# Later checks of converted slices, two slots for the first quarter sums, and undivided reciprocal copies in a fused attention and Fourier-mixing kernel

## The chip, the cores and the metric

The kernel runs on one core of one Trainium2 chip. The metric is the device time of one execution in microseconds; the number for a kernel is the median of its runs. One execution was also recorded by the hardware profiler, which gives the trace and the profile.

## The reference, cut to what matters

Two blocks follow each other. The first is an attention in which a query sees only the keys of its own hash bucket; the second mixes by a Fourier transform over sequence and channels, normalizes, and applies two dense layers.

```python
# attention: q, k, v are (4, 8, 768, 64), proj is (64, 6)
q_bits = (einsum('bhsd,dk->bhsk', q, proj) > 0); k_bits = ...
mask = q_bucket[:, :, :, None] == k_bucket[:, :, None, :]
scores = where(mask, q @ k.T / sqrt(64), -1e9)
attn = exp(scores - max); attn = attn / (sum(attn) + 1e-9)
x = (attn @ v), heads side by side            # (4, 768, 512)
# mixing: w_ch1 is (512, 2048), w_ch2 is (2048, 512), given as 64-bit floats
u = x + real(fft(fft(x, axis=1), axis=2))
un = (u - mean(u)) / sqrt(var(u) + 1e-6)
out = u + relu(un @ w_ch1) @ w_ch2
```

## The kernel before, in words

There are four batches, and each has four pairs of heads, numbered n = 0 to 15. While the attention of batch b runs, the mixing of batch b - 1 runs in its gaps: the main loop (L1567 on) steps through `attention(b)` chunk by chunk and advances the generator `other`, which is `mix(b - 1)`, in proportion. So TensorE has matmuls of both at hand. The part that the change touches is the attention of batch 1 (pairs 4 to 7) beside the mixing of batch 0, and within it the preparation of the weights that all later batches use.

**Attention of a pair.** The keys come in six chunks of 128 (`scores`, `weights`, `weigh`, `values`). For a chunk TensorE makes two score tiles (L905), ScalarE takes their exponential into one of two buffers `pk0` and `pk1` (L916), VectorE multiplies each head by the bucket mask (L930), VectorE adds the chunk to the running sum `acc` (L1026, in `tally`), and TensorE multiplies by the values (L941). When a pair's six chunks are through, `scale` makes the reciprocals of the row sums: a matmul over ones (L960), a transpose (L967), an addition and a reciprocal (L969, L970), eight small copies on ScalarE that put the reciprocals into place (L978, tile `rr`), another transpose (L983) and a multiplication of the pair's output (L987). In batch 1 the eight copies are made in two groups of four, one chunk apart, and each group is put behind the last exponential, mask or sum that was issued.

**Anchors.** `in_turn()` issues what stands under it after the instructions that `done_by` remembers, one for ScalarE and one for VectorE. Else a scheduler of the framework orders the instructions of all batches but the first by its own priorities. The first batch's attention has its order written out.

**The first dense layer.** `mlp7` uses a seven-product scheme in place of eight. The 2048 columns of `w1` are taken as 8 steps f, and for each f `quarters(f)` makes four sums of quarters of `w1` on VectorE: s1 (L1249), s2 (L1250), s3 (L1251) and s4 (L1252) in four slots of the tile `tq`, and stores the seven factors to DRAM (tile `ad`, L1254 and L1255) for the later batches. `inner` (L1466 on) then makes the seven products of f: A11 and A12 into bank p1, S2 into p6, S1 and S4 into p5, S3 and A22 into p7 (all L1456). Two PSUM banks serve these four names in turn in batches 0 to 2, so each product waits for a copy of ScalarE: L1478 and L1485 read p1, L1481 reads p6, L1488 and L1497 read p5, L1493 and L1505 read p7. VectorE adds them up (L1482, L1489, L1494, L1498, L1506), ScalarE applies the rectifier (L1495, L1499, L1507). `quarters(f + 1)` is called at the end of step f.

**The second dense layer.** `outer7` does the same for the other layer, three times two row blocks j for each half of the hidden columns (L1335), with sums on VectorE (L1320, L1321, L1355, L1363, L1347, L1381 to L1387) and copies on ScalarE (L1354, L1365, L1368); its temporaries are slots 0 to 2 and 3 to 5 of the same tile `tq`, in turn.

**The conversion of w2.** `weights2` runs beside the mixing of batch 0 and turns 16 slices of 64-bit `w_ch2` into 32-bit floats. `Arrival.convert(i)` calls `narrow`: two VectorE operations on the high words (L639, L643), one ScalarE operation on the low words (L647), two additions on VectorE (L652), and then a check on ScalarE of whether any value is too small (L654 and L655, which ends with the reading of an accumulated sum). The check overwrites the raw slice. Then `fetch(i + 2)` loads the next slice into the same one of two raw slots, from the GpSimd queue (L704). After every second slice VectorE makes four sums of the pair (L1301 to L1304), and after eight slices the half is stored to DRAM (`bd`, L1306).

Of the kernel before, what the change touches and what calls it, by code (L numbers as in the profile page):

```python
# [20 lines left out]
P = 128  # L21
# [464 lines left out]
def _main(  # L486
# [141 lines left out]
    def narrow(dst, raw, col, low=None):  # L628


        lo, hi = (raw[..., i] for i in range(2))
        t = lo.bitcast(F32)
        if low is None:

            low, t = lo, hi.bitcast(F32)
        di = dst.bitcast(I32)


        nc.vector.tensor_scalar(  # L639
            di, hi, 3, (1 << 30) - 1,  # L640
            op0=ALU.logical_shift_left, op1=ALU.bitwise_and,
        )
        nc.vector.scalar_tensor_tensor(  # L643
            di, hi, -(1 << 30), di, op0=ALU.bitwise_and, op1=ALU.bitwise_or
        )

        nc.scalar.activation(low, lo.bitcast(U32), AF.Copy, scale=2.0**-29)  # L647
        if len(di.shape) == 2:
            nc.vector.tensor_tensor(di, di, low, op=ALU.add)
        else:  # L650
            for i in range(di.shape[1]):
                nc.vector.tensor_tensor(di[:, i], di[:, i], low[:, i], op=ALU.add)  # L652

        nc.scalar.activation(t, hi, AF.Abs)  # L654
        nc.scalar.activation(  # L655
            t, t, AF.Relu, bias=least, scale=-1.0, accum_out=strange[:, col : col + 1]
        )
# [33 lines left out]
    class Arrival:  # L691


        def __init__(self, slices, raws, col, queue):
            self.slices, self.raws, self.col, self.queue = slices, raws, col, queue
            self.wide = slices[0][1].dtype == I64
# [14 lines left out]
        def convert(self, i, low=None):  # L711
            if self.wide:
# [6 lines left out]
                narrow(dst, raw, self.col + i, low)  # L719
            self.fetch(i + self.depth)  # L720
# [226 lines left out]
    def scale(n, oos, sums):  # L947
# [25 lines left out]
        apart = NPAIR <= n < TWO  # L973
        for g in range(2):
            with in_turn() if apart else nullcontext():
                for i in range(4):
                    j = 2 * g + i // 2
                    nc.scalar.copy(  # L978
                        rr[32 * i : 32 * i + 32, g], rc[32 * j : 32 * j + 32]
                    )  # L980
            if apart and g == 0:
                yield
# [6 lines left out]
    def attention(b):  # L989
# [11 lines left out]
        for t in range(NPAIR):  # L1001
# [12 lines left out]
            def tally(c, pk, sums):  # L1014
# [8 lines left out]
                else:  # L1023

                    for g in (0, 1) if b == 0 else (slice(0, 2),):
                        done_by[ET.DVE] = nc.vector.tensor_tensor(  # L1026
# [41 lines left out]
        for sc in scales:  # L1068
            if next(sc, True) is None:
                yield  # L1070
                next(sc, None)
# [170 lines left out]
    def quarters(f):  # L1242

        st = tq[:, 0:4].rearrange("p i (k m) -> p i k m", m=P)
# [3 lines left out]
        s2, s1, s3, s4 = (st[:, i] for i in range(4))  # L1248
# [6 lines left out]
        nc.sync.dma_start(ad[f, 3:7].rearrange("i p k m -> p i k m"), st)  # L1255
# [17 lines left out]

    def weights2():
# [13 lines left out]
        arrival = Arrival(slices, [zt2[:, i] for i in range(2)], NDC * DFF // WC, nc.gpsimd)  # L1288
        for half in range(2):
# [4 lines left out]
            for i in range(HF):  # L1294
                with in_turn():
                    arrival.convert(half * HF + i)
                yield
                if i % 2:
                    b11, b21, b22, t4, t1, t2, t3 = (q[:, i // 2] for q in right7)
                    with in_turn():  # L1300
                        nc.vector.tensor_tensor(t3, b22, t1, op=ALU.subtract)  # L1301
                        nc.vector.tensor_tensor(t1, t1, b11, op=ALU.subtract)
                        nc.vector.tensor_tensor(t2, b22, t1, op=ALU.subtract)
                        nc.vector.tensor_tensor(t4, b21, t2, op=ALU.subtract)  # L1304
# [93 lines left out]
    def mlp7(b):  # L1398
# [46 lines left out]
        def product(i, ps, start=True):  # L1445
            n = done[0]
            left = ring[n % NR]
            if b == 0:
                f = n // 7
                if i >= S2:  # L1450
                    left = tq[:, i - S2].rearrange("p (k m) -> p k m", m=P)
# [61 lines left out]
        for half in range(2):  # L1513
            if b == 0 and half:
                quarters(HF // 2)
            for i, _ in enumerate(inner(half)):
                if b == 0 and half and i % 3 < 2:
                    next(arrival2, None)
                yield
# [9 lines left out]
    def after(n, one, two):  # L1529

        for i, _ in enumerate(one):
            if i >= n and (i - n) % 2 == 0:
                next(two, None)
            yield
# [124 lines left out]
```

## Time and profile before

| what | number |
|---|---|
| median of three runs | 1079.54 us |
| lowest and highest | 1077.59 and 1079.67 us |
| the profiled execution | 1079.54 us, of which the span is 1077.8 us |
| TensorE busy | 1034.6 us (96%) |
| VectorE busy | 786.7 us (73%) |
| ScalarE busy | 500.4 us (46%) |
| GpSimd busy | 59.3 us (5%) |
| check of a w2 slice, three instructions of L654 and L655 | 688, 776 and 190 ns |
| one reciprocal copy (L978) | 197 ns |
| one quarter sum or pair sum (L1249 to L1252, L1301 to L1304) | 417 to 420 ns |

The profile names engines PE (TensorE matmul), PEld (its weight load), DVE (VectorE), ACT (ScalarE), POOL (GpSimd) and SP (SyncE). A row gives a source line, an operation, the tiles written and read, and a duration; what stands in brackets is how long the engine was idle before it, and which instruction ended the wait. Instructions overlap at their ends, so rows that follow each other start closer together than their durations say.

### The profile page before, as it was taken

What the parts mean: (1) busy time and instruction counts of PE and PEld (TensorE: products, weight loads), DVE (VectorE), ACT (ScalarE), POOL (GpSimd) and SP (SyncE); (2) the same over time, 40 slices, a digit from 0 to 9 for tenths busy, and PEclk for the clock granted to TensorE, in tenths of its full rate; (3) what the DMA queues carried; (4) which work ended last, traced back from release to release, by engine and by line L of the source; (5) the groups of instructions that cost most, each with busy time, mean ns of one, the idle gap of its engine ahead of it and who ended that gap; (6) DMA issues with size and microseconds to landing.
All of it is one profiled execution on the core that took longest, in us unless ns stands there. A gap on an engine that the chain in (4) does not pass through costs nothing.

```text
span 1077.8 us, 14130 instructions
## 1 busy us (share of the span) xinstructions
PE 1034.6 (96%) x4933; PEld 633.4 (59%) x4933; DVE 786.7 (73%) x1336; ACT 500.4 (46%) x1055; POOL 59.3 (5%) x132
## 2 busy tenths in 40 slices
PE   7989899999999999999999999999999999999997
PEld 3333364447644585545664575645675579668576
DVE  5899969896789977777858876776856875644353
ACT  6988554762287323455336424354325522440420
POOL 0000000011000020010000020010000012200000
PEclk9999999999999999999999999999999999999998
DMA  8764452370154461224062233222033204222301
GB/s 200 206 141 78 99 143 54 122 237 9 29 131 169 136 187 37 52 64 88 11 191 73 64 104 116 50 66 66 15 111 96 69 23 173 61 78 90 125 20 42
DMA packets 175710, 103.13 MB, mean 96 GB/s; under 512 B 129552, under 2 KB 162960, under 8 KB 175632
## 3 DMA queue, kind: packets, MB, share of 16 engines
q1 hardware_dynamic: 169840, 88.65, 30.6%
q0 software_dynamic: 4224, 13.11, 3.7%
q8 instruction: 41, 0.67, 0.3%
q10 hardware_dynamic: 1568, 0.39, 0.2%
q14 instruction: 37, 0.30, 0.1%
HBM read 81.14 MB, written 20.97 MB: 95 GB/s over the span
## 4 chain that ended last, share of the span: by engine, by line
PE 72%; DVE 17%; ACT 6%; issue 2%; DMA 1%; SPq 1%; DVEq 0%; ACTq 0%
PE o L1335 26%; PE h_p L1456 22%; PE oo L941 8%; PE sc L905 7%; DVE acc L1026 3%; DVE pk L930 2%; PE cs L1147 2%; ACT pk L916 2%; PE A L1176 2%; PE B L1176 1%; DMA kn<-in_k_dram 1%; ACT rr L978 1%; DVE x L1190 1%; PE sum L960 1%; SPq L576 1%
## 5 line engine op out<-in xcount | busy, mean ns | idle before, releaser
L1335 PE MATMUL o<-w,h 128*128 128x256 f32 x1152 | 260.0, 383 | 0.8 <-DVE w L1347 0.6
L1335 PEld LDWEIGHTS o<-w,h 128*128 128x128 f32 x1152 | 217.8, 191 | 41.8 <-issue 6.5
L916 ACT ACTIVATE pk<-sc 128x768 f32<-128x768 f32 x192 | 147.4, 809 | 78.2 <-PE oo L941 33.3
L1456 PE MATMUL h_p<-x,w 128*128 128x384 f32 x448 | 164.5, 494 | 3.1 <-ACT h L1478 1.6
L905 PE MATMUL sc<-qt,kt 64*128 64x384 f32 x768 | 154.9, 505 | 3.1 <-ACT pk L916 2.8
L930 DVE SCALAR_TENSOR_TENSOR pk<-qb,kb,pk 128x768 f32<-128x768 bf16 x132 | 128.7, 1012 | 39.0 <-ACT pk L916 38.4
L941 PE MATMUL oo<-pk,vn 128*64 128x385 f32 (+1 forms) x768 | 146.4, 495 | 1.1 <-DVE pk L930 0.6
L1456 PEld LDWEIGHTS h_p<-x,w 128*128 128x128 f32 x448 | 82.0, 190 | 69.3 <-issue 9.9
L1026 DVE TENSOR_TENSOR acc<-acc,pk 128x1536 f32<-128x1536 f32 (+1 forms) x72 | 105.8, 1483 | 5.3 <-ACT pk L916 5.1
L1456 PE MATMUL h_p<-w 128*128 128x384 f32 x288 | 106.1, 490 | 0.1
L941 PEld LDWEIGHTS oo<-pk,vn 128*64 128x64 f32 x768 | 50.5, 136 | 87.0 <-issue 72.6
L905 PEld LDWEIGHTS sc<-qt,kt 64*128 64x128 f32 x768 | 66.5, 187 | 55.7 <-issue 18.4
L1456 PEld LDWEIGHTS h_p<-w 128*128 128x128 f32 x288 | 53.6, 190 | 39.6 <-ACT w L1493 2.4
L1365 ACT COPY tq<-o 128x256 f32<-128x256 f32 x24 | 8.9, 373 | 104.8 <-PE o L1335 104.8
L1347 DVE SCALAR_TENSOR_TENSOR w<-o,rs,w 128x256 f32<-128x256 f32 x56 | 26.6, 479 | 41.2 <-PE o L1335 41.2
L1335 PE MATMUL o<-w 128*128 128x256 f32 x176 | 42.2, 383 | 0.2 <-DVE w L1347 0.2
L1489 DVE TENSOR_TENSOR h<-h 128x384 f32<-128x384 f32 x32 | 17.8, 555 | 29.6 <-ACT h L1488 29.6
L1085 POOL DMA_DIRECT2D out_dram<-w x30 | 16.4, 548 | 407.6 <-issue 314.6
L1335 PEld LDWEIGHTS o<-w 128*128 128x128 f32 x176 | 32.9, 190 | 7.5 <-DVE w L1347 1.2
L1354 ACT COPY tq<-o 128x256 f32<-128x256 f32 x24 | 8.8, 368 | 60.3 <-PE o L1335 60.1
L1381 DVE TENSOR_TENSOR tq<-tq,o 128x256 f32<-128x256 f32 x24 | 10.0, 418 | 36.4 <-PE o L1335 36.4
L1482 DVE TENSOR_TENSOR h<-h 128x384 f32<-128x384 f32 x32 | 17.7, 552 | 21.8 <-ACT h L1481 21.7
(170 smaller groups left out, 1334.5 us busy)
## 6 DMA issues: line engine op xcount, KB each, us to landing
w<-ad SPq DMA_DIRECT2D x168, 128.0 KB, 2.0
w<-bd SPq DMA_DIRECT2D x42, 512.0 KB, 4.4
zraw<-in_moe_w_ch_dram POOLq DMA_DIRECT2D x16, 512.0 KB, 4.4
bd<-w SPq DMA_DIRECT2D x14, 512.0 KB, 3.3
vn<-in_v_dram SPq DMA_DIRECT2D x32, 192.0 KB, 3.5
qn<-in_q_dram SPq DMA_DIRECT2D x120, 48.0 KB, 2.4
kn<-in_k_dram SPq DMA_DIRECT2D x60, 96.0 KB, 3.0
zraw<-in_moe_w_ch_dram SPq DMA_DIRECT2D x8, 512.0 KB, 7.4
```

The costliest lines, as they stand in the source:

```text
L905: last[0] = nc.tensor.matmul(ps[:, h, 0:HALF], kt[rows, ks], qt[rows, qs], start=kb is not None, stop=True,)
L916: done_by[ET.Activation] = nc.scalar.activation(pk[:, g, :, 0:HALF], ps[:, :, 0:HALF], AF.Exp, scale=SCALE)
L930: done_by[ET.DVE] = nc.vector.scalar_tensor_tensor(w, qb[:, h].rearrange("p (g s) -> p g s", g=2), kb[:, h, c : c + 1], w, op0=ALU.is_equa ...
L941: oo = nc.tensor.matmul(oos[g][h * D : (h + 1) * D, 0:w], nat["v", n][:, (2 * c + h) * D : (2 * c + h + 1) * D], pk[:, g, h, 0:w], start=( ...
L1026: done_by[ET.DVE] = nc.vector.tensor_tensor(acc[:, g], (first if c == 1 else acc)[:, g], new[:, g], op=ALU.add,)
L1147: nc.tensor.matmul(ps[:, pc + 2 * lo : pc + 2 * hi - 1 : 2], z[:, cp, pc, par, t * P : (t + 1) * P], ch[:, cp, pc, lo:hi], start=(cp == 0) ...
L1176: nc.tensor.matmul(ps[:, cols], F[:, par, k, t, j * P : (j + 1) * P], sq[:, t, k, cols], start=(t == 0), stop=(t == 1),)
L1335: nc.tensor.matmul(ps, a[:, r], right7[i][:, r], start=start and r == 0, stop=r == HF // 2 - 1, skip_group_check=not start,)
L1347: nc.vector.scalar_tensor_tensor(t[:, cols], src, r, t[:, cols], op0=ALU.mult, op1=ALU.add)
L1456: nc.tensor.matmul(ps, left[:, k], right[i][:, k], start=start and k == 0, stop=k == 1, skip_group_check=not start,)
L1482: done_by[ET.DVE] = nc.vector.tensor_tensor(c21, c12, c21, op=ALU.add)
L1489: done_by[ET.DVE] = nc.vector.tensor_tensor(c22, c21, c22, op=ALU.add)
```

## The change

It has three parts. The check of a converted `w2` slice and the fetch that follows it are no longer made with the conversion but kept as `rest` and made by `settle()`, which is called before the next conversion or at the mixing step after it; the four sums of a pair of slices lose their anchor. The first two sums of `quarters` use slots 0 and 1 of `tq` for even f and slots 4 and 5 for odd f, where the four sums of an odd f are stored by two transfers in place of one. And the eight reciprocal copies of a pair of batch 1 are issued in one step and without an anchor, as they are in the other batches; the additions into `acc` are no longer remembered in `done_by`.

```diff
@@ -651,10 +651,13 @@
             for i in range(di.shape[1]):
                 nc.vector.tensor_tensor(di[:, i], di[:, i], low[:, i], op=ALU.add)
 
-        nc.scalar.activation(t, hi, AF.Abs)
-        nc.scalar.activation(
-            t, t, AF.Relu, bias=least, scale=-1.0, accum_out=strange[:, col : col + 1]
-        )
+        def check():
+            nc.scalar.activation(t, hi, AF.Abs)
+            nc.scalar.activation(
+                t, t, AF.Relu, bias=least, scale=-1.0, accum_out=strange[:, col : col + 1]
+            )
+
+        return check
 
     def average(f):
 
@@ -693,6 +696,7 @@
 
         def __init__(self, slices, raws, col, queue):
             self.slices, self.raws, self.col, self.queue = slices, raws, col, queue
+            self.rest = None
             self.wide = slices[0][1].dtype == I64
             self.depth = len(raws) if self.wide else 4
 
@@ -708,7 +712,8 @@
                         dst, src if len(dst.shape) == 2 else src.rearrange("p (s n) -> p s n", n=n)
                     )
 
-        def convert(self, i, low=None):
+        def convert(self, i, low=None, later=False):
+            check = None
             if self.wide:
                 dst = self.slices[i][0]
                 raw = self.raws[i % self.depth].bitcast(I32)
@@ -716,8 +721,23 @@
                     raw = raw.rearrange("p (n w) -> p n w", w=2)
                 else:
                     raw = raw.rearrange("p (s n w) -> p s n w", w=2, n=dst.shape[-1])
-                narrow(dst, raw, self.col + i, low)
-            self.fetch(i + self.depth)
+                check = narrow(dst, raw, self.col + i, low)
+
+            def rest():
+                if check:
+                    check()
+                self.fetch(i + self.depth)
+
+            if later:
+                self.rest = rest
+            else:
+                rest()
+
+        def settle(self):
+            if self.rest:
+                with in_turn():
+                    self.rest()
+                self.rest = None
 
     def weights1():
         slices = [
@@ -970,16 +990,10 @@
         nc.vector.reciprocal(rc, rc)
         yield
         rr = wt([P, 2, HALF // 32], F32, "rr", f"rr{n}")
-        apart = NPAIR <= n < TWO
         for g in range(2):
-            with in_turn() if apart else nullcontext():
-                for i in range(4):
-                    j = 2 * g + i // 2
-                    nc.scalar.copy(
-                        rr[32 * i : 32 * i + 32, g], rc[32 * j : 32 * j + 32]
-                    )
-            if apart and g == 0:
-                yield
+            for i in range(4):
+                j = 2 * g + i // 2
+                nc.scalar.copy(rr[32 * i : 32 * i + 32, g], rc[32 * j : 32 * j + 32])
         nc.vector.transpose(
             rt.rearrange("p (j i) -> p j i", i=32),
             rr.rearrange("p g j -> p (g j)")[:, :, None].broadcast_to([P, S // 32, 32]),
@@ -1023,7 +1037,7 @@
                 else:
 
                     for g in (0, 1) if b == 0 else (slice(0, 2),):
-                        done_by[ET.DVE] = nc.vector.tensor_tensor(
+                        nc.vector.tensor_tensor(
                             acc[:, g], (first if c == 1 else acc)[:, g], new[:, g],
                             op=ALU.add,
                         )
@@ -1066,9 +1080,7 @@
         while pending:
             finish()
         for sc in scales:
-            if next(sc, True) is None:
-                yield
-                next(sc, None)
+            next(sc, None)
 
 
     HW = HALF // 2
@@ -1241,18 +1253,23 @@
 
     def quarters(f):
 
-        st = tq[:, 0:4].rearrange("p i (k m) -> p i k m", m=P)
+        st = tq.rearrange("p i (k m) -> p i k m", m=P)
         (a11, a12), (a21, a22) = (
             [w1[:, c : c + 2, r * P : (r + 1) * P] for c in (0, 2)] for r in (f, f + HF)
         )
-        s2, s1, s3, s4 = (st[:, i] for i in range(4))
+        at = f % 2 * 4
+        s2, s1, s3, s4 = (st[:, i] for i in (at, at + 1, 2, 3))
         nc.vector.tensor_tensor(s1, a21, a22, op=ALU.add)
         nc.vector.tensor_tensor(s2, s1, a11, op=ALU.subtract)
         nc.vector.tensor_tensor(s3, a11, a21, op=ALU.subtract)
         nc.vector.tensor_tensor(s4, a12, s2, op=ALU.subtract)
         for i, a in ((A11, a11), (A12, a12), (A22, a22)):
             nc.sync.dma_start(ad[f, i], a)
-        nc.sync.dma_start(ad[f, 3:7].rearrange("i p k m -> p i k m"), st)
+        parts = ((3, 7, 0),) if at == 0 else ((3, 5, at), (5, 7, 2))
+        for i0, i1, j in parts:
+            nc.sync.dma_start(
+                ad[f, i0:i1].rearrange("i p k m -> p i k m"), st[:, j : j + i1 - i0]
+            )
 
 
 
@@ -1271,6 +1288,8 @@
         for i in range(2)
     ]
 
+    second = []
+
     def weights2():
 
         slices = []
@@ -1286,22 +1305,24 @@
                          moe_w_ch2[c * P : (c + 1) * P, :])
                     )
         arrival = Arrival(slices, [zt2[:, i] for i in range(2)], NDC * DFF // WC, nc.gpsimd)
+        second.append(arrival)
         for half in range(2):
             if half == 0:
                 for i in range(arrival.depth):
                     arrival.fetch(i)
                 yield
             for i in range(HF):
+                arrival.settle()
                 with in_turn():
-                    arrival.convert(half * HF + i)
+                    arrival.convert(half * HF + i, later=True)
                 yield
                 if i % 2:
                     b11, b21, b22, t4, t1, t2, t3 = (q[:, i // 2] for q in right7)
-                    with in_turn():
-                        nc.vector.tensor_tensor(t3, b22, t1, op=ALU.subtract)
-                        nc.vector.tensor_tensor(t1, t1, b11, op=ALU.subtract)
-                        nc.vector.tensor_tensor(t2, b22, t1, op=ALU.subtract)
-                        nc.vector.tensor_tensor(t4, b21, t2, op=ALU.subtract)
+                    nc.vector.tensor_tensor(t3, b22, t1, op=ALU.subtract)
+                    nc.vector.tensor_tensor(t1, t1, b11, op=ALU.subtract)
+                    nc.vector.tensor_tensor(t2, b22, t1, op=ALU.subtract)
+                    nc.vector.tensor_tensor(t4, b21, t2, op=ALU.subtract)
+            arrival.settle()
             for i in range(7):
                 nc.sync.dma_start(bd[half, i], right7[i])
             if half == 0:
@@ -1448,7 +1469,8 @@
             if b == 0:
                 f = n // 7
                 if i >= S2:
-                    left = tq[:, i - S2].rearrange("p (k m) -> p k m", m=P)
+                    j = i - S2 + (4 if f % 2 and i in (S2, S1) else 0)
+                    left = tq[:, j].rearrange("p (k m) -> p k m", m=P)
                 else:
                     c, r = (0 if i == A11 else 2), (f + HF if i == A22 else f)
                     left = w1[:, c : c + 2, r * P : (r + 1) * P]
@@ -1516,6 +1538,8 @@
             for i, _ in enumerate(inner(half)):
                 if b == 0 and half and i % 3 < 2:
                     next(arrival2, None)
+                elif b == 0 and half:
+                    second[0].settle()
                 yield
             if b == 0 and half == 0:
                 for T in range(3):
@@ -1531,6 +1555,8 @@
         for i, _ in enumerate(one):
             if i >= n and (i - n) % 2 == 0:
                 next(two, None)
+            elif i >= n:
+                second[0].settle()
             yield
         for _ in two:
             pass
```

## The prediction

> **What bounds the kernel now.** I read the page first, then the busy time by stretch of the span, then TensorE's own timeline with the waits ahead of its instructions, and last ScalarE's and VectorE's timelines around those waits. The profiled execution took 1079.54 us, which is also the median of the three runs; its span is 1077.8, so 1.74 us lie around it.
>
> ```profile
> span 1077.8 us, 14130 instructions
> PE 1034.6 (96%) x4933; PEld 633.4 (59%) x4933; DVE 786.7 (73%) x1336; ACT 500.4 (46%) x1055; POOL 59.3 (5%) x132
> ```
> TensorE (PE) is the bound; its idle time is all that a change of order can win. The diff touches only the second batch's attention beside the first batch's mixing. From the two instruction orders (no time is in them), TensorE's differs from the first `un0_3` transpose (about 172 us) up to `cs1_0_0` (about 400 us), and from there the rest is the same. Busy time by stretch (PE, PEld, DVE, ACT, POOL, then clock, DMA share, GB/s):
>
> ```profile
> 148.00:400.00 252.00, 241.10 (x1062) 144.45 (x1059) 217.31 (x399) 129.08 (x274) 22.82 (x41) 0.99 0.41 119
> 300.00:361.00 61.00, 56.80 (x234) 28.52 (x230) 57.84 (x114) 42.94 (x93) 3.27 (x6) 1.00 0.51 162
> 377.00:378.00 1.00, 1.00 (x4) 0.73 (x4) 1.00 (x3) 0.02 (x1) 0.00 (x0) 0.50 0.66 108
> ```
> In 148 to 400 TensorE idles 10.9 us; from 300 to 361 VectorE (57.84 of 61) is as much the bound as TensorE; and at 377 TensorE ran at half clock. TensorE's waits (in brackets: idle before, and who ended it):
>
> ```profile
> 174.02 0.92 PE L905 MATMUL sc<-qt,kt 64*128 64x384 f32 x4 [0.48 <-ACT pk L916]
> ...
> 197.44 1.56 PE L1456 MATMUL h_p<-x,w 128*128 128x384 f32 x4 [1.12 <-ACT h L1478]
> ...
> 205.94 1.56 PE L1456 MATMUL h_p<-x,w 128*128 128x384 f32 x4 [0.81 <-ACT w L1505]
> ...
> 241.49 3.72 PE L1335 MATMUL o<-w,h 128*128 128x256 f32 x16
> ...
> 326.68 1.56 PE L1456 MATMUL h_p<-bt,tq 128*128 128x384 f32 x4 [0.99 <-ACT h L1481]
> ...
> 337.58 1.53 PE L1456 MATMUL h_p<-bt,tq 128*128 128x384 f32 x4 [1.25 <-DVE tq L1250]
> ...
> 361.25 5.45 PE L1335 MATMUL o<-w,h 128*128 128x256 f32 x24 [0.55 <-DVE w L1347]
> ...
> 375.11 1.05 PE L905 MATMUL sc<-qt,kt 64*128 64x384 f32 x4 [1.59 <-ACT pk L916]
> 376.09 5.23 PE L1335 MATMUL o<-w,h 128*128 128x256 f32 x16
> ```
> ScalarE (ACT) just ahead of the first and the last of them:
>
> ```profile
> 195.20 0.68 ACT L654 ACTIVATE zraw<-zraw 128x512 f32<-128x512 int32 x1
> ...
> 196.18 0.75 ACT L655 ACTIVATE zraw<-zraw,least 128x512 f32<-128x512 f32 x1
> ...
> 196.91 0.47 ACT L1478 COPY h<-h_p 128x384 f32<-128x384 f32 x1
> ...
> 372.56 1.67 ACT L978 COPY rr<-rc 32x12 f32<-32x12 f32 x8
> 374.25 1.51 ACT L916 ACTIVATE pk<-sc 128x768 f32<-128x768 f32 x2
> ```
> The check (L654, L655) stands ahead of the copy that TensorE waits for at 197.44; and eight reciprocal copies of pair 7 stand between two exponentials of pair 8, for which TensorE waits 0.27 and then 1.59 us.
>
> **The change part by part.** No arithmetic is added or removed; only orders, two slots and four more stores.
>
> *A. The end of the stage.* The dropped `yield` and anchors put pair 7's eight copies (1.67 us) right after `o0_1_1_0`'s copy, and pair 8's first scores behind the last product of the stage. The waits of 0.27 and 1.59 go. With them goes a slow spell: by the rows, 16 matmuls at L1335 take 5.23 us at 376.09 and 3.72 at 241.49, 1.5 us more, and the four score matmuls ahead 0.1 more, so 1.6. What is late next: the third score tile still needs the first one's exponential, the wait of 0.27, so +0.3. Sum −1.86 −1.6 +0.3 = −3.2. Ends: −3.5 (no wait), −1.6 (the spell comes elsewhere).
> [...]
>
> *B. Second run of w1's products (290 to 361).* The 0.99 at 326.68 is L1481 standing behind L654, L655 and the reading of the sum (1.5 us from 324.69 to 326.17); in the changed order L1481 stands ahead of that check. The 1.25 at 337.58 is the second quarter sum L1250, queued behind a slice's conversion; with own slots for odd quarters both first sums stand 41 and 29 VectorE instructions earlier. The 0.55 at 361.25 is VectorE being late at the end of its full stretch; four sums of a converted pair (L1301 to L1304, 4 × 0.335 by their starts) and the multiply of pair 6 (0.95) move ahead of the `acc` sum at 312.22, partly into idle time (2.13 us before the mask at 309.46), and at the end a mask, an `ef` and an L1320 fall behind the L1347 that TensorE waited for. Together −2.8. Against it: pair 6's copies now run as eight before the second exponential, 0.8 later, and I find L643, with the check that waits for it and L1493 behind that, 0.3 later at the wait of 0.88. So −2.5; since VectorE has 3.2 us of air in 61, I let 0.5 of it come back as other waits: −2.0. Ends: −2.8 and +0.5.
>
> *C. The first deferred checks.* In the changed order L1478 and L1481 stand ahead of the check's 1.3 us (0.56 + 0.74 by starts), so the 1.12 at 197.44 goes. The 0.81 at 205.94 stays: L1505 is now behind L1495, L1499 and half a check. −1.1, ends −1.9 and 0.
>
> *D. The start (168 to 189).* The four sums of a converted pair, no longer anchored, now stand before pair 4's sum transpose (L967), which had 0.59 of idle: 1.34 − 0.59, so 0.75 later. Queued behind it: the reciprocal, the eight copies, the exponential L916 behind them, then score tile `sc5_1_3`, which the new order also puts ahead of most transposes. I follow it: TensorE stops at 172.75 until about 174.5, a gap of 1.75 where 0.72 and 0.48 stood; then the mask is late by nothing (L1250 and L1249 of quarter 0 left this place, 0.67) but less work lies before it. At the first S1 product I get 189.2 against 188.41: +0.8. Ends: 0, and +2.4 if a half-clock spell of 1.6 follows the gap.
>
> *E. Pair 5's copies (236 to 250).* Four copies more (0.82) before the second exponential, then transpose L983 (0.90) and multiply L987 (0.87) ahead of the masks: the second mask ends 1.7 later. The L1335 products behind it wait, but they waited for VectorE (0.19 + 0.23 and stretched rows) up to 249.68 anyway, and the new order has 2.9 us of scores and values to put there. +0.6, ends 0 and +1.7.
>
> *At nothing.* Fetches: the refill of a raw slot is issued behind the check, so GpSimd's queue runs later; a fetch lands 4.4 us after issue, the tightest was issued at 318.13 and used at 323.30, so the cover is 0.7 us, and each us beyond costs VectorE as much (0 to +0.5, inside B's end). SyncE's queue gets four more stores (0.38 us each): ahead of loads of q and k used over 10 us later. An odd quarter's store must land (3.5 us) before its slots are written again two quarters on, over 25 us later.
>
> Sum: −3.2 −2.0 −1.1 +0.8 +0.6 = −4.9; 1079.54 − 4.9 = **1074.6 us**.
>
> **Rivals.** About 0.2% (2.2 us) is what a measurement of this kernel can tell from no change: faster is below 1077.4, slower above 1081.7.
> 1. *Slower: a pair's closing moves in front of its next masks.* Pairs 5, 6 and 7 each get eight copies in one run before an exponential (0.82 later) and L983 with L987 before the masks (1.77): 2.6 us a pair where nothing covers it, and 1.6 more where the gap drops the clock. For: VectorE is full, and D and E show such gaps. Against: TensorE has products at hand, and pair 7's scores moved away. With all three uncovered and two spells, +7.8 +3.2, against −3.2 −2.0 −1.1: +4.7, 1084. It decides from two uncovered pairs with two spells on (+5.2 +3.2 −6.3 = +2.1).
> 2. *No change: VectorE gives it back.* Of B nothing is left (+0.5), C is lost to the VectorE sums behind it (0), D and E hold (+1.4), A holds: −1.3, 1078.2. For: 57.84 of 61 busy, and for the first two slices of the second half (298 to 304) the check stands in the very same place of ScalarE's order, so there the change doesn't do what it says.
> 3. *The spell is not the gap's.* Of A only −1.6: 1079.54 − 3.3 = 1076.2. For: gaps of 1.60 and 1.93 at 48 and 76 us were followed by full clock.
>
> **How the numbers follow.** Forecast 0.46 and rival 3 0.18, both faster: 0.64. Rival 2: 0.20. Rival 1: 0.16. The likeliest is the forecast, 1074.6. Range: the low end has A at −3.5, B at −2.8, C at −1.9, D and E at 0, −8.2: 1071.3. The high end has A −3.2, B +0.5, C 0, D +2.4, E +1.7, +1.4: 1081.0. Beyond lies most of rival 1 and a little below.
>
> **What would show it.** Right: no half-clock slice near the end of the stage; score tiles of pair 8 after the last L1335 of batch 0 with at most 0.3 us of wait; no wait for L1481 or L1250 near 325 and 336; `cs1_0_0` near 395 in place of 400.15, and from there the same distances. Wrong: a slice with clock 0.50 near 174 or 240, waits over 1.5 us for L916 at pairs 5 or 6, VectorE idle on raw slices, or `cs1_0_0` at 399 or later. If the time is lost after `cs1_0_0`, the premise that the rest only shifts is wrong.

## The result and the profile after

The changed kernel takes 1081.68 us (median of 22 runs, 1080.59 to 1082.87) where the kernel before took 1078.06 (22 runs, 1077.37 to 1081.12): a ratio of 1.0029, interval [1.0023, 1.0036]. By this ratio it is slower by some 3.1 us; the two medians lie 3.6 apart. 1074.6 was predicted, with 1071.3 to 1081.0 as the range. The forecast took its 4.9 us off 1079.54, the median of three runs, which is 1.5 above the median of 22.

Its profiled execution took 1080.94 us, span 1079.1. The head of its page:

```profile
span 1079.1 us, 14130 instructions
...
PE 1033.5 (96%) x4933; PEld 632.2 (59%) x4933; DVE 788.8 (73%) x1336; ACT 498.8 (46%) x1055; POOL 59.1 (5%) x132
```

The same stretches as before (PE, PEld, DVE, ACT, POOL, then clock, DMA share, GB/s):

```profile
148.00:400.00 252.00, 239.88 (x1066) 143.31 (x1062) 215.58 (x398) 126.09 (x273) 24.09 (x44) 1.00 0.43 123
300.00:361.00 61.00, 56.07 (x228) 28.42 (x226) 58.55 (x115) 42.14 (x92) 3.65 (x7) 1.00 0.53 161
377.00:378.00 1.00, 0.92 (x4) 0.68 (x4) 1.00 (x2) 0.00 (x0) 0.00 (x0) 1.00 0.66 104
```

The half clock at 377 is gone, yet TensorE is idle for 12.1 us of the 252 where it was for 10.9, and in 300 to 361 VectorE is fuller than before (58.55 of 61). TensorE's timeline, the waits in brackets (line numbers in a kernel's rows are those of that kernel: L925, L936, L950, L961, L1356, L1478 and L1515 here are L905, L916, L930, L941, L1335, L1456 and L1493 of the kernel before):

```profile
138.53 1.16 PE L1159 MATMUL cs<-ch,z 128*128 128x127 f32 x8 [1.26 <-DVE bt L860]
...
170.78 0.92 PE L1188 MATMUL B<-sq,F 128*128 128x193 f32 x4 [0.69 <-DVE rt L987]
173.33 0.92 PE L925 MATMUL sc<-qt,kt 64*128 64x384 f32 x4 [0.65 <-ACT pk L936]
175.71 0.92 PE L925 MATMUL sc<-qt,kt 64*128 64x384 f32 x4 [1.10 <-ACT pk L936]
179.86 1.51 PE L961 MATMUL oo<-pk,vn 128*64 128x385 f32 x4 [0.94 <-DVE pk L950]
...
190.52 1.45 PE L1478 MATMUL h_p<-bt,tq 128*128 128x384 f32 x4
...
206.90 1.56 PE L1478 MATMUL h_p<-x,w 128*128 128x384 f32 x4 [0.86 <-DVE bt L860]
...
240.61 0.92 PE L925 MATMUL sc<-qt,kt 64*128 64x384 f32 x4 [1.02 <-ACT pk L936]
...
243.49 1.51 PE L961 MATMUL oo<-pk,vn 128*64 128x385 f32 x6 [0.94 <-DVE pk L950]
244.93 5.64 PE L1356 MATMUL o<-w,h 128*128 128x256 f32 x24
...
319.97 1.56 PE L1478 MATMUL h_p<-zraw,w 128*128 128x384 f32 x4 [1.67 <-ACT w L1515]
...
338.47 1.56 PE L1478 MATMUL h_p<-x,w 128*128 128x384 f32 x4 [1.45 <-ACT h L1519]
...
347.62 1.56 PE L1478 MATMUL h_p<-bt,tq 128*128 128x384 f32 x4 [1.10 <-DVE bt L860]
...
398.82 1.62 PE L925 MATMUL sc<-qt,kt 64*128 64x384 f32 x8 [0.27 <-ACT pk L936]
400.36 1.81 PE L1159 MATMUL cs<-ch,z 128*128 128x129 f32 x11
```

The waits that the change aimed at are gone (1.12 at 197, 0.99, 1.25 and 0.55 between 326 and 361, 1.59 at 375), and others of the same size stand in their place. Of the prediction's signs of being right three came: no half clock near the end of the stage, at most 0.27 us of wait for pair 8's scores, no wait for L1481 or L1250. The fourth did not: `cs1_0_0` stands at 400.36, and 399 or later was named as a sign of being wrong. Cut at points that both kernels have, the two profiled executions compare so (us):

| stretch | before | after | difference |
|---|---|---|---|
| up to the first matmul | 5.10 | 4.86 | -0.24 |
| first matmul to pair 4's sum | 162.44 | 163.21 | +0.77 |
| the stage: pair 4's sum to `cs1_0_0` | 232.61 | 232.29 | -0.32 |
| `cs1_0_0` to the last matmul | 669.36 | 669.55 | +0.19 |
| to the end of the last store's issue | 3.17 | 3.35 | +0.18 |
| from there to the span's end | 5.09 | 5.81 | +0.72 |
| around the span | 1.77 | 1.87 | +0.10 |

That is +1.40, the difference of the two executions (1079.54, 1080.94). Most of the rest is a half-clock stretch near 377 us that the execution before happened to have and the one after had not: e7, whose stage has the same waits as before's, ran it at full clock in 230.98, so an estimate of its cost is 1.63. Without it the difference is 1.40 + 1.63 = 3.0 us, and the stage alone is +1.3. The fastest runs of the two kernels, 1077.37 and 1080.59, lie 3.2 apart.

### The profile page after: what moved, and what is told of

Its sections match the earlier page's. It is cut to its first block, busy times and chain, and to the rows that moved or that the text cites. A ratio compares the mean times of both kernels' runs of the same rounds, so it can differ in the third digit from the quotient of the medians.

```text
span 1079.1 us, 14130 instructions
## 1 busy us (share of the span) xinstructions
PE 1033.5 (96%) x4933; PEld 632.2 (59%) x4933; DVE 788.8 (73%) x1336; ACT 498.8 (46%) x1055; POOL 59.1 (5%) x132
## 4 chain that ended last, share of the span: by engine, by line
PE 70%; DVE 16%; ACT 7%; issue 3%; SPq 2%; DMA 1%; DVEq 0%; ACTq 0%
PE o L1356 27%; PE h_p L1478 20%; PE oo L961 8%; PE sc L925 7%; DVE acc L1040 3%; DVE pk L950 3%; PE cs L1159 2%; ACT pk L936 2%; PE A L1188 2%; PE B L1188 1%; SPq L576 1%; DMA kn<-in_k_dram 1%; DVE x L1202 1%; ACT rr L996 1%; DVE w L652 1%
## 5 line engine op out<-in xcount | busy, mean ns | idle before, releaser
L1356 PE MATMUL o<-w,h 128*128 128x256 f32 x1152 | 257.9, 381 | 0.3 <-DVE w L1368 0.3
L1356 PEld LDWEIGHTS o<-w,h 128*128 128x128 f32 x1152 | 216.9, 190 | 40.2 <-issue 5.8
L936 ACT ACTIVATE pk<-sc 128x768 f32<-128x768 f32 x192 | 147.0, 808 | 81.1 <-PE oo L961 33.3
L1478 PE MATMUL h_p<-x,w 128*128 128x384 f32 x448 | 164.2, 494 | 3.1 <-ACT h L1519 1.4
L925 PE MATMUL sc<-qt,kt 64*128 64x384 f32 x768 | 154.6, 505 | 3.6 <-ACT pk L936 3.3
L950 DVE SCALAR_TENSOR_TENSOR pk<-qb,kb,pk 128x768 f32<-128x768 bf16 x132 | 128.7, 1012 | 32.8 <-ACT pk L936 32.7
L961 PE MATMUL oo<-pk,vn 128*64 128x385 f32 (+1 forms) x768 | 146.7, 495 | 2.6 <-DVE pk L950 2.0
L1478 PEld LDWEIGHTS h_p<-x,w 128*128 128x128 f32 x448 | 81.9, 190 | 69.1 <-issue 9.3
L1478 PE MATMUL h_p<-w 128*128 128x384 f32 x288 | 106.1, 490 | 0.1
L961 PEld LDWEIGHTS oo<-pk,vn 128*64 128x64 f32 x768 | 50.5, 136 | 88.4 <-issue 72.4
L925 PEld LDWEIGHTS sc<-qt,kt 64*128 64x128 f32 x768 | 66.5, 187 | 56.2 <-issue 20.1
L1478 PEld LDWEIGHTS h_p<-w 128*128 128x128 f32 x288 | 53.6, 190 | 39.6 <-ACT w L1515 2.4
L1356 PE MATMUL o<-w 128*128 128x256 f32 x176 | 42.1, 382 | 0.0
L1356 PEld LDWEIGHTS o<-w 128*128 128x128 f32 x176 | 33.0, 190 | 6.9 <-issue 1.1
```

The source lines that it names most:

```text
L925: last[0] = nc.tensor.matmul(ps[:, h, 0:HALF], kt[rows, ks], qt[rows, qs], start=kb is not None, stop=True,)
L936: done_by[ET.Activation] = nc.scalar.activation(pk[:, g, :, 0:HALF], ps[:, :, 0:HALF], AF.Exp, scale=SCALE)
L950: done_by[ET.DVE] = nc.vector.scalar_tensor_tensor(w, qb[:, h].rearrange("p (g s) -> p g s", g=2), kb[:, h, c : c + 1], w, op0=ALU.is_equa ...
L961: oo = nc.tensor.matmul(oos[g][h * D : (h + 1) * D, 0:w], nat["v", n][:, (2 * c + h) * D : (2 * c + h + 1) * D], pk[:, g, h, 0:w], start=( ...
L1356: nc.tensor.matmul(ps, a[:, r], right7[i][:, r], start=start and r == 0, stop=r == HF // 2 - 1, skip_group_check=not start,)
L1478: nc.tensor.matmul(ps, left[:, k], right[i][:, k], start=start and k == 0, stop=k == 1, skip_group_check=not start,)
```

## The experiments

Each label was timed against the kernel before, beside it on one chip; us against before are the ratio's excess times before's median. e1 to e4, e5 to e8 and e9 to e12 were timed on three different chips, so labels of different groups are compared by their ratios. Most intervals are some 2 us wide, so a difference of 1 us between two labels is not shown by the times alone; where one is read below, the traces carry it. From each trace: the stretch from the first matmul to pair 4's sum, the stage, the half-clock windows in the stage (stretches of 3.41 us, as the one from 375.77 in before, in which the profile shows TensorE's granted clock at half), and the delay at SyncE's 844th record (explained with e6 and e7).

| kernel | ratio and interval | us | to pair 4's sum | stage | half clock | record 844 |
|---|---|---|---|---|---|---|
| before | | | 162.44 | 232.61 | 1 | none |
| after | 1.0029 [1.0023, 1.0036] | +3.1 | 163.21 | 232.29 | 0 | 0.64 |
| e1 | 0.9998 [0.9987, 1.0009] | -0.2 | 162.65 | 233.08 | 1 | none |
| e2 | 1.0001 [0.9991, 1.0011] | +0.1 | 163.37 | 232.96 | 2 | none |
| e3 | 1.0011 [1.0002, 1.0020] | +1.2 | 163.51 | 231.39 | 0 | 0.79 |
| e4 | 1.0019 [1.0009, 1.0029] | +2.1 | 163.44 | 231.34 | 0 | 0.70 |
| e5 | 1.0030 [1.0019, 1.0041] | +3.2 | 163.88 | 233.30 | 1 | 0.92 |
| e6 | 1.0025 [1.0016, 1.0033] | +2.7 | 164.21 | 232.42 | 0 | none |
| e7 | 1.0004 [0.9995, 1.0014] | +0.4 | 162.54 | 230.98 | 0 | 1.10 |
| e8 | 1.0022 [1.0011, 1.0033] | +2.4 | 163.30 | 231.33 | 0 | 0.84 |
| e9 | 1.0017 [1.0009, 1.0026] | +1.8 | 161.91 | 232.90 | 0 | none |
| e10 | 0.9986 [0.9977, 0.9994] | -1.5 | 162.19 | 228.97 | 0 | none |
| e11 | 1.0005 [0.9996, 1.0014] | +0.5 | 162.60 | 232.86 | 1 | none |
| e12 | 0.9992 [0.9984, 1.0001] | -0.9 | 162.20 | 230.19 | 0 | none |

**One part alone (e1 to e3), and all but one (e4).** e1 is the kernel before with the copies undivided; e2 has the later checks and fetches and the free sums of a pair of slices; e3 has the two slots with their extra stores; e4 is the changed kernel with the copies in two parts.

```diff
 e1 (e4 puts these lines back into the changed kernel)
-            with in_turn() if apart else nullcontext():
...
-            if apart and g == 0:
-                yield
...
-                        done_by[ET.DVE] = nc.vector.tensor_tensor(
+                        nc.vector.tensor_tensor(
...
 e2: check(), rest() and settle() of the change, and
-                    with in_turn():
                         nc.vector.tensor_tensor(t3, b22, t1, op=ALU.subtract)
...
 e3
+        at = f % 2 * 4
+        s2, s1, s3, s4 = (st[:, i] for i in (at, at + 1, 2, 3))
...
+        parts = ((3, 7, 0),) if at == 0 else ((3, 5, at), (5, 7, 2))
```

> The kernel before with only the reciprocal copies changed: eight in one step, no anchor, acc sums not remembered. Theory 1 (a pair's closing in one piece costs: eight copies 0.82 us later in front of an exponential, transpose and multiply 1.77 us in front of the next masks): it carries the loss alone, 2 to 5 us over the kernel before, with TensorE waits for masks or exponentials near 174, 240 and 305. Theory 2 (the four sums of a converted pair, now without anchor, make pair 4's closing late and so lose the time): this kernel has them anchored, so it stands within 1 us of the kernel before.

> The kernel before with only the checks and fetches made one step later and the four sums unanchored. Theory 1: a gain of 1 to 2 us, since the wait of 1.12 for L1478's copy and that of 0.99 for L1481's go. Theory 2: a loss of 2 to 4 us, with the gap near 174 us (1.1 in the changed kernel) in its trace.

> The kernel before with only two slots for the first two quarter sums (and the split store). Theory 1: a gain of about 1.2 us, the wait for the second quarter sum near 337 us gone; waits elsewhere unchanged. Theory 2: no more than 1 us either way, VectorE giving the wait back at its next place.

> The changed kernel with the copies again in two parts (so the kernel before with later checks and two slots). Theory 1: 1.5 to 3.5 us below the kernel before, and so 5 or more below the changed one. Theory 2: 2 us or more above the kernel before, as the changed one.

No part carries the loss alone: -0.2, +0.1 and +1.2 add up to +1.1, so some 2 of the 3.1 us come only in company, with about 1 us of doubt on each of these numbers. Theory 1 of e1 and of e4 falls; e2 has neither the gain nor the loss expected of it, and e3 loses 1.2 where theory 1 had it gain as much. e1 shows no difference in time, but its trace has two waits that are in none of the kernels with divided copies (before, e2, e4, e10 and e12 have at most 0.19 there, for the second row of scores), and that all with undivided ones have, the changed kernel at 240.61 and 243.49:

```profile
238.82 0.92 PE L905 MATMUL sc<-qt,kt 64*128 64x384 f32 x4 [1.02 <-ACT pk L916]
...
241.70 1.51 PE L941 MATMUL oo<-pk,vn 128*64 128x385 f32 x6 [0.94 <-DVE pk L930]
```

So the undivided copies are what makes part E cost. With the divided copies put back (e4) the stage is 231.34 in place of 232.29, 1.0 less, and the times agree with it (+2.1 for +3.1), though their intervals overlap. e2's stage is the shortest of the four once its two half-clock windows are allowed for: 232.96 less 2 x 1.63 is an estimate of 229.7, 1.3 under e7's 230.98. Its median shows nothing of that: the traced execution spent it on those windows and on a late pair 4's sum, and what took it in the others is not shown. e3 and e4 showed something unforeseen, as the changed kernel had, a pair 4's sum some 1 us late and an end 0.7 us longer, which the next runs take up.

**The changed kernel again (e5), its odd quarters in one store (e6), and four more stores alone (e7).**

```diff
 e6
-        parts = ((3, 7, 0),) if at == 0 else ((3, 5, at), (5, 7, 2))
...
+        j = f % 2 * 2
+        nc.sync.dma_start(ad[f, 3:7].rearrange("i p k m -> p i k m"), st[:, j : j + 4])
...
 e7
-        nc.sync.dma_start(ad[f, 3:7].rearrange("i p k m -> p i k m"), st)
+        for i0, i1 in ((3, 5), (5, 7)) if f % 2 else ((3, 7),):
+            nc.sync.dma_start(
+                ad[f, i0:i1].rearrange("i p k m -> p i k m"), st[:, i0 - 3 : i1 - 3]
+            )
```

> The changed kernel again, unaltered, beside the next three. In its first trace, beside that of before: VectorE's two sums of f = 1 (L1261 and L1262) stand near 136 in place of 191, and TensorE waits 1.26 for bt at 138.5 where it waited 0.65; SyncE's last DRAIN stands 0.64 after the instruction ahead of it where it stood 0.05; and the stage from pair 4's sum to the first cs of batch 1 took 232.3 without a half-clock window, where before took 232.6 with one, which is worth 1.7. Theory 1 (three separate losses: early sums, end of SyncE's program, stage): all three again in this trace, each within 0.3 us, and a time 2.5 to 3.6 us above before. Theory 2 (the loss is half-clock windows that happened to be absent from the one trace): some windows at clock 0.50 between 170 and 400, the stage 234 or more, and the end as short as in before.

> The changed kernel, but the four sums of an odd f are stored by one transfer again: they lie side by side in slots 2 to 5, and DRAM holds them in that order, which the later batches' loads take into account. SyncE has as many instructions as in before. Theory 1: SyncE's last DRAIN follows at 0.05 again, 0.6 to 0.7 us less from the last store to the end of the span, everything else as in the changed kernel, so 0.7 us less than it in all (about +2.4 against before). Rival (the longer end belongs to the slots or to where the last output lands, not to the number of SyncE's instructions): the end stays 0.65 longer.

> The kernel before, but the four sums of an odd f are stored by two transfers in place of one, as in the changed kernel; nothing else. Theory 1: the last DRAIN of SyncE comes 0.6 to 0.8 late, the rest of the trace stays as in before: +0.7 us. Rival: no change in time (the end as short as in before), because the longer end comes from something else. A second rival, that the four stores cost time within the stage by holding up SyncE's queue: the stage 1 us longer or more.

e5 repeats the three losses, with a half-clock window of its own on top, so theory 2 falls. That window in its trace (the third figure from the end is the clock):

```profile
177.00:180.00 3.00, 3.00 (x14) 1.75 (x12) 3.00 (x6) 2.05 (x4) 0.00 (x0) 0.51 0.07 23
```

The end of the program shows how four stores that nobody waits for can cost. SyncE's last records (number, us, operation, gap to the record ahead of it; the page leaves these out of busy time):

```
kernel  number  us       operation        gap
before  842     1077.20  DRAIN            0.07
before  843     1077.70  EVENT_SEMAPHORE  0.49
after   843     1077.49  DRAIN            0.04
after   844     1078.15  DRAIN            0.64
...
after   847     1079.01  EVENT_SEMAPHORE  0.49
e6      840     1079.63  DRAIN            0.08
e6      841     1080.13  EVENT_SEMAPHORE  0.49
e7      843     1075.44  EVENT_SEMAPHORE  0.06
e7      844     1076.57  EVENT_SEMAPHORE  1.10
```

Every kernel with the four stores has 847 or 850 records on SyncE and a gap of 0.64 to 1.10 ahead of number 844, whatever instruction that is; every kernel without them ends at 840 to 843 and has none. The kernel before ends one record short of it. From the last store's issue to the end it is 5.70 to 6.14 us with the stores, 5.01 to 5.23 without. The times say too little (+0.4 for e7, between -0.5 and +1.5; +2.7 for e6 where the changed kernel has +3.1 and +3.2), but e7's trace shows the delay alone, with the waits of the stage unchanged, and e6's the changed kernel without the delay. What SyncE waits for at that place no view names, and no run shows what causes it.

**The sums of a pair anchored (e8), and those of f = 1 (e9).**

```diff
 e8
+                    with in_turn():
                         nc.vector.tensor_tensor(t3, b22, t1, op=ALU.subtract)
...
 e9 (with e6's one store)
+        with in_turn() if f == 1 else nullcontext():
             nc.vector.tensor_tensor(s1, a21, a22, op=ALU.add)
```

> The changed kernel, but the four sums of a pair of w2 slices are made under in_turn() again. In the changed kernel they stand ahead of pair 4's sum transpose, and TensorE waits 0.69, 0.65, 1.10 and 0.94 at 170.8, 173.3, 175.7 and 179.9, where before had 0.72, 0.48 and twice 0.29; the S1 product of f = 0 comes 1.6 us later from the sum than in before. Theory 1 (the free sums are what makes the start of the stage late): the product comes within 0.4 us of before's distance, and 1.0 to 1.6 us are won against the changed kernel. Rival (the start is late because the eight copies in one run and the moved score tile are, and the sums ran in idle time of VectorE): the waits stay within 0.3, and the time within 0.5 us of the changed kernel.

> The changed kernel with two things undone: an odd quarter is stored in one transfer (as in e6), and the four sums of f = 1 are made under in_turn(), so that its first two do not run at 136 ahead of the bt that TensorE waits for. Theory 1 (the early sums put everything behind them off by their own 2 x 0.42 us): the wait at 138.5 is 0.65 again, the fifth sum comes 0.8 us earlier after the first matmul (162.5 without the half-clock windows' effect), the end as in e6, the stage as in the changed kernel (232.3); +1.5 against before. Rival (VectorE's order there costs nothing, since TensorE's later waits take it up): the fifth sum at 163.2 or more, +2.3 to +2.5 as e6.

VectorE's timeline of the changed kernel shows both places:

```profile
135.47 0.42 DVE L1262 TENSOR_TENSOR tq<-w 128x256 f32<-128x256 f32 x1
135.92 0.42 DVE L1263 TENSOR_TENSOR tq<-tq,w 128x256 f32<-128x256 f32 x1
136.26 1.75 DVE L1040 TENSOR_TENSOR acc<-acc,pk 128x1536 f32<-128x1536 f32 x1
137.93 0.55 DVE L860 TENSOR_SCALAR bt<-bits 128x384 bf16<-128x384 f32 x1
...
168.43 0.42 DVE L1321 TENSOR_TENSOR w<-w 128x256 f32<-128x256 f32 x1
168.89 0.43 DVE L1322 TENSOR_TENSOR w<-w 128x256 f32<-128x256 f32 x1
169.35 0.42 DVE L1323 TENSOR_TENSOR w<-w 128x256 f32<-128x256 f32 x1
169.81 0.42 DVE L1324 TENSOR_TENSOR w<-w 128x256 f32<-128x256 f32 x1
170.15 0.58 DVE L987 STREAM_TRANSPOSE rt<-sum 128x384 f32<-128x384 f32 x1
```

The first two sums of f = 1 have slots of their own and no anchor, so nothing holds them: they run at 135.5, 55 us before they are due, ahead of the `bt` that TensorE waits for at 138.53 (1.26, where it was 0.65). In e9 they are gone from there, the wait is 0.66, and pair 4's sum comes at 161.9; among the traces with no half-clock window ahead of that sum, e3 and e4 with the early sums have 163.5 and 163.4, e7, e9, e10, e11 and e12 without them 161.9 to 162.6. That is 0.8 to 1.6 us; the times agree with it (+1.8 for e6's +2.7), though their intervals overlap. e9's stage has 0.5 more than e6's, with a new wait of 1.00 at 197.18. e8 gives the start of the stage back, the waits 0.72, 0.48 and 0.64 in place of 0.69, 0.65, 1.10 and 0.94, and its stage is 1.0 shorter, as theory 1 had it (+2.4 for +3.1 by the times, again with overlapping intervals). But it has the gap of pair 8's scores again:

```profile
376.62 0.92 PE L925 MATMUL sc<-qt,kt 64*128 64x384 f32 x4 [1.68 <-ACT pk L936]
```

**Later checks, with only the first pair's sums held (e10), with all held (e11), and the whole change with its costs taken out (e12).**

```diff
 e10 (e2 and)
+                    with in_turn() if half == 0 and i == 1 else nullcontext():
                         nc.vector.tensor_tensor(t3, b22, t1, op=ALU.subtract)
...
 e11 (e2 and)
+                    with in_turn():
                         nc.vector.tensor_tensor(t3, b22, t1, op=ALU.subtract)
...
 e12: e4 with e6's one store, e9's and e10's anchors
```

> The kernel before with the later checks and fetches alone (e2), but the four sums of the first pair of w2 slices are made under in_turn(), those of the other seven pairs stay free. Theory 1 (in the start of the stage only the free sums cost, and the later checks do save the waits for the copies and the gap at the end): waits at 171 to 181 as in before (1.8 in place of e2's 2.8), no wait above 0.5 between 370 and the first cs of batch 1, the stage 228.5 without half-clock windows where before's is 230.9 without them; by the time 1 to 2.4 us faster than before. Rival (VectorE is full, what is won at the start comes back as other waits): the stage 229.5 or more, and no difference in time.

> The kernel before with the later checks and fetches alone, and the sums of all eight pairs under in_turn() as in before. Theory 1: the start as in e10; if the checks alone are what takes the gap of pair 8's scores away, no wait above 0.5 between 370 and the first cs of batch 1, and 1 to 2 us faster than before. Rival (the free sums took that gap away, as e8, where they are anchored and the gap of 1.68 is back, suggests): a wait of about 1.6 near 375, the stage 230 or more, no gain.

> Later checks and two slots, without the three things that the runs found to cost: odd quarters in one store, the sums of f = 1 and of the first pair of w2 slices under in_turn(), the reciprocal copies in two parts as in before. Theory 1: no early sums (fifth sum at 162.5), the end of SyncE's program as in before, the start of the stage as in before, so the stage 230.3 to 230.6 (e4's 231.3 less 1.0) and 0 to 1 us faster than before, slower than e10, since the slots bring new waits for L1515 and L1519. Rival (the slots do save the waits for the quarter sums once nothing else stands in their way): 1.5 us or more faster than before, and faster than e10.

e10 is faster than the kernel before, 1076.52 us against 1078.22, ratio 0.9986 [0.9977, 0.9994], and so than the changed one. Its stage took 228.97, 2.0 less than e7's at full clock; TensorE is idle in it for 8.6 us, where it was for 10.9 in before. Its waits:

```profile
171.43 0.52 PE L1222 MATMUL un<-ident,x 128*128 128x128 f32 x3 [0.72 <-DVE x L1210]
173.53 0.92 PE L925 MATMUL sc<-qt,kt 64*128 64x384 f32 x4 [0.47 <-ACT pk L936]
178.09 1.51 PE L961 MATMUL oo<-pk,vn 128*64 128x385 f32 x4 [0.29 <-DVE pk L950]
...
315.00 1.56 PE L1481 MATMUL h_p<-zraw,w 128*128 128x384 f32 x4 [1.07 <-ACT w L1518]
...
340.52 0.52 PE L856 MATMUL bits<-qt,pj 128*32 128x384 f32 x2 [1.89 <-ACT h L1506]
343.40 1.56 PE L1481 MATMUL h_p<-bt,tq 128*128 128x384 f32 x4 [1.19 <-DVE bt L860]
...
394.48 1.61 PE L925 MATMUL sc<-qt,kt 64*128 64x384 f32 x8 [0.27 <-ACT pk L936]
```

The start is before's, the end has only 0.27, the 1.12 and 0.81 near 200 have become one of 0.32, and between 300 and 362 nothing is won (1.07, 1.89 and 1.19 for before's 0.88, 0.99, 1.25 and 0.55). e11 has no gap at the end either, so the sums alone don't decide it; holding all eight pairs cost a wait of 2.08 at 206.0 and the gain, and a half-clock window came behind it (clock 0.50 from 207 to 209). Why e8 has the gap and e11 hasn't stays open; e8 has the undivided copies and the slots too. e12 did as theory 1 had it: no faster than e10, its stage 1.2 longer, so there is no sign that the slots bring anything.

## Why the prediction was wrong, step by step

Without the half-clock spell the forecast for the stage was -3.3, and +1.3 was measured. Part B is the step that failed most, by 2.4 us; E was short by 1.0 and D by 0.8. Outside the stage the sum lacked two terms, +0.8 and +0.7, and it counted in full, as a gain of 1.6, a spell that only part of the executions have.

**A, the end of the stage: the waits went, but not for the reason given, and the clock was wrong as a gain.** The waits went from 1.86 to 0.53 (0.26 and 0.27 are left), -1.33 where -1.56 was counted. The prediction put this down to the dropped `yield` and anchors of the reciprocal copies. e1 has these alone and keeps both waits; e2, which has before's copies and the later checks, has only 0.27, because pair 8's scores stand behind the last products of batch 0:

```profile
392.79 5.34 PE L1359 MATMUL o<-w,h 128*128 128x256 f32 x24
398.07 1.56 PE L925 MATMUL sc<-qt,kt 64*128 64x384 f32 x8
399.90 1.61 PE L925 MATMUL sc<-qt,kt 64*128 64x384 f32 x8 [0.27 <-ACT pk L936]
```

That they would stand there had been read from the instruction order, but the part of the change that puts them there was named wrongly, so the size is right by luck. Later checks alone are enough in the kernel before (e11, with the sums held, has no such gap), yet e8 has them among the other parts and keeps it; why stays open.

The half-clock spell did vanish in this trace, but it was no fixed part of the time. Five traces have the gap of 1.6 to 1.7 us (before, e1, e3, e7, e8); two of them fell to half clock behind it (mean clock from 376 to 379: 0.50 in before, 0.54 in e1, 1.00 in e3, e7 and e8). TensorE ahead of and behind the gap in e1, then in e3:

```profile
376.00 1.46 PE L905 MATMUL sc<-qt,kt 64*128 64x384 f32 x4 [1.59 <-ACT pk L916]
377.38 4.82 PE L1327 MATMUL o<-w,h 128*128 128x256 f32 x16
```

```profile
376.59 0.92 PE L905 MATMUL sc<-qt,kt 64*128 64x384 f32 x4 [1.59 <-ACT pk L916]
377.43 3.72 PE L1340 MATMUL o<-w,h 128*128 128x256 f32 x16
```

The same gap, and 16 matmuls take 4.82 or 3.72. Taking 1.6 off was right for the profiled execution and too much for a typical one, since only 2 of these 5 traces have the spell: 2 in 5 times 1.63 is an estimate of 0.7. The mean clocks on record fit that roughly: 31 of the 98 runs of the kernel before beside the experiments have one of 0.994 or less, as the profiled execution has. Rival 3 was right that the gap alone doesn't make the spell.

**B, the second run of w1's products: the mechanism failed.** -2.0 was forecast; the waits of 0.25 and more between 290 and 362 went from 4.46 to 4.81, +0.35. The three waits went as forecast, and VectorE, full before and after, was late elsewhere. ScalarE ahead of the largest new wait:

```profile
318.89 0.68 ACT L655 ACTIVATE zraw<-zraw 128x512 f32<-128x512 int32 x1 [2.06 <-DVE w L643]
319.46 0.46 ACT L1515 COPY w<-h_p 128x384 f32<-128x384 f32 x1
```

L655, the first operation of a check, waits for VectorE's L643, and the copy that TensorE needs waits behind it. L643 comes late because pair 6's copies run together and its transpose, masks and multiply follow without a break from 311.64. The prediction saw this wait (0.88 before) and gave it 0.3; it grew by 0.79. e4, with the copies divided, has 1.07 there, so the undivided copies make 0.6 of the 0.79. At 338.47 it is VectorE again: the copy L1519 stands on ScalarE behind a rectifier that waits for L1516, and that stands behind four sums and two masks. Here rival 2 was right. Over the traces this stretch of 61 us is hard to move: its waits above 0.25 sum to 3.8 to 4.8 in before, after, e1, e2, e3, e4, e10 and e12, whatever is put first.

**C, the first deferred checks: right.** 1.12 and 0.81 became 0.86, -1.07 for a forecast -1.1. The 1.12 went as told. The wait that "stays" is another one: it was for ScalarE's L1505, and now it is for VectorE's `bt` (L860).

**D, the start: right place, half the size.** The waits from 171 to 180 went from 1.78 to 3.38, +1.6 for +0.8; the S1 product stands at 190.52, where 189.2 was forecast and before had 188.41 (0.53 of it came from ahead of the stage). The four sums were taken at 0.335 each, 1.34 in all, less 0.59 of idle. In before 0.335 is the distance of a sum from another instruction put between two of them; here they stand one behind the other, start 0.46 apart (0.45 for the one such pair in before, at 228.78), and the transpose L987 follows 1.72 after the first: 1.13 late, not 0.75. e2 divides the +1.6: its waits there are 2.82, so the free sums make 1.0, and the undivided copies of the changed kernel the rest, through the last of the four waits (0.94 for e2's 0.38).

**E, pair 5's copies: right place, well under half the size.** +0.6 was forecast and +1.6 measured (0.75 of waits became 2.35; 0.14 of the 0.75 is too short for the timeline to print). The products that were to cover it stand behind these scores and values in TensorE's order (at 244.93, the values at 243.49) and can't. Rival 1's mechanism is this one, true for pair 5 and in part for pairs 4 and 6, without any spell.

Together -1.33 + 0.35 - 1.07 + 1.6 + 1.6 = +1.15, close to what the stage lost at full clock (+1.3, 232.29 against e7's 230.98); the forecast without the spell was -3.3.

**What the sum lacked.** Two terms had no place in it, because all parts were looked for inside the stage. The early sums of f = 1 (+0.8 ahead of pair 4's sum) were told as "41 and 29 VectorE instructions earlier" and never asked who stands behind them there. The four stores were put "at nothing" by what their queue holds up; the end of SyncE's program was not looked at, and cost +0.7. The premise that all behind `cs1_0_0` only shifts held (+0.19 over 669 us).

## What to carry to other kernels

An instruction freed of its anchor or its slot can go as early as its data let it, and on a full engine somebody stands behind it there: look at the new place, not only at the wait that it leaves. Where VectorE was busy for 57 of 61 us, removing TensorE's waits one by one moved them to the next one; what paid here (e10) was to free the checks and most of the sums, and to hold the four sums that stood ahead of what TensorE waited for. A wait that is gone has not been explained yet: run each part alone to see which one took it away. And before a half-clock spell is counted as a gain, see whether it belongs to the kernel or to that one execution.

## What the runs showed of the hardware

Between 24 and 1060 us TensorE's granted clock stands at half in two stretches in before, from 116.36 and from 375.77, and in one in after, from 116.84; each is 3.41 us long. In the 3.41 us ahead of them TensorE was busy for 1.06, 1.57 and 1.38 us, and the longest waits there were 1.60, 1.59 and 1.60. Such a stretch wasn't always followed by half clock: from 72.50 to 75.90 after's TensorE was busy for 1.46 of 3.40 us, with a wait of 1.94, and the clock stood at 1.00 there and from 75.90 to 79.30. Nor did the same waits always end alike. In before TensorE waits 1.60 at 114.01 and 1.51 at 116.59, and the 8 matmuls at 116.59 take 1.93; in e4 it waits 1.62 and 1.51 at the same two instructions (114.61 and 117.18), and the 8 matmuls take 1.06. For the gap near 375 the five traces with it show the same, 16 matmuls behind it in 5.23 us (before), 4.82 (e1) and 3.72 (e3, e7, e8). What decides between the two isn't shown.

The delay at SyncE's 844th record was not expected: 0.64 to 1.10 us, in all six programs with more than 843 records on SyncE and in none of the eight with fewer than 844. Its cause stays open.
